# Two units of a rational activation in one instruction, on the steps that read SBUF alone

## The chip, the cores and the metric

The kernel runs on one NeuronCore of a Trainium2 chip. The metric is the device time of one execution in microseconds (us); a run's time is the median over its executions. The engines are TensorE (PE, with its weight loads PEld), VectorE (DVE), ScalarE (ACT) and GpSimd (POOL); SyncE (SP) only issues transfers. Each engine works through its own row of instructions in order. SBUF is the working memory with 128 partitions, PSUM holds matmul results in banks of 512 fp32 columns.

## The reference

A delta-rule attention (4 batches, 8 heads, 768 time steps, head size 48) is followed by a two-layer network with a rational activation (384 to 2048 to 384 columns, 3072 tokens):

```python
for t in range(S):
    y[:, :, t] = np.einsum('bhd,bhde->bhe', q[:, :, t], state)
    v_old = np.einsum('bhde,bhd->bhe', state, kt)
    state = state + bt * np.einsum('bhd,bhe->bhde', kt, vt - v_old)
...
h = x @ w_in
h2 = h * h
h3 = h2 * h
P = a[0] + a[1] * h + a[2] * h2 + a[3] * h3
Q = 1.0 + np.abs(b[0]) * np.abs(h) + np.abs(b[1]) * h2
g = P / (Q + 1e-06)
return g @ w_out
```

## The kernel before, in words

Time is cut into 12 chunks of 64 steps. For each chunk the attention is solved in blocks (the inverse of a triangular matrix in many small VectorE steps, the products on TensorE) and gives 256 tokens. They are transposed into `xT`, and the network runs on them.

The network walks over the hidden layer in units of two tiles of 128 hidden columns. A unit is 2 x 256 = 512 columns on 128 partitions, exactly one PSUM bank, and there are 8 units (`NU`) in a chunk, 96 in all. A unit n passes four functions:

- `hidden(n)`: 18 matmuls into one of two PSUM banks (`ps_h`, tile `ph`). Numbers are carried as pairs of fp16 (high and low part), so each product is three passes.
- `numerator(n)`: ScalarE computes `u = A3*h + a2` (L827) and `z = |B1*h|` (L829) from the bank, VectorE computes `u = h*u` (L830), `w = (z + B0)*h` (L832) and `u = (u + A1)*h` (L834), reading the bank each time. After L834 the bank is free. ScalarE then takes `w = |w|` (L833). In half the units of the chunks 2 to 10 GpSimd adds A0 to u (L838, `by_pool`).
- `quotient(n)`: ScalarE forms 1/Q as `exp(-ln(w + Q0))` (L845, L846, tile `r`). VectorE makes the high part `g = (u + A0)*r` in fp16 (L851, or L849 where GpSimd has added A0), then `w = (w + Q0)*g` (L852) and the remainder `u = u + A0 - w` (L856; in the `by_pool` units L854 on GpSimd). GpSimd makes the low part `u*r` (L857). All of these read SBUF only.
- `accumulate(n)`: 12 matmuls of g with `w_out` into `po` (L872). At the end of a chunk ScalarE scales `po` into `ob` (L886), and SP sends it out (L894).

The tiles u, r, w and g come from four tags, `mu`, `mr`, `mw`, `mg`, with three buffers (`MB`) each.

Before the first unit the weights are read as 64-bit floats and made into fp16 pairs (`load_in`, `load_out`, `to_f32`): SP loads a piece (L322) into a buffer of the tags mw, mu, mr in turn, ScalarE takes the absolute value (L325, into a buffer of `mg`), GpSimd clamps it (L326), VectorE shifts and joins the bits (L327, two L334). One scale is found for each unit.

The order of the instructions on each engine is fixed when the program is built, by a scheduler that sorts by priority and by a model of the times; the main loop interleaves one unit's numerator, the unit before's quotient and a piece of the attention of later chunks.

## Time and profile before

| | |
|---|---|
| median of 3 runs | 870.52 us (869.87 to 877.41) |
| span of the profiled execution | 875.0 us |
| VectorE busy | 797.9 us, 91% |
| TensorE busy | 629.4 us, 72% (weight loads 494.5 us) |
| ScalarE busy | 550.9 us, 63% |
| GpSimd busy | 469.5 us, 54% |
| first and last L827 | at 150.5 and 858.0 us |

Of the profiled execution only the span is known, from its first instruction to its last; it lies between the median and the slowest of the three runs. The rows of a page give a line, the engine, the operation, what it writes and reads, its shape and its count; behind the bar stand the busy time in us and the mean length of one in ns, then the idle time of the engine just before it and what ended that. The lengths of neighbours on VectorE overlap a little, so how long an instruction holds the queue is read from the next one's start.

### The profile page before, as it was taken

To read this page: it belongs to the slowest core of one execution; us is meant where nothing else is said; L and a number is where in the kernel's file an instruction comes from. 1 tells how busy PE (TensorE), PEld (TensorE's weight loads), DVE (VectorE), ACT (ScalarE), POOL (GpSimd) and SP (SyncE) were. 2 spreads that over 40 slices of the span, in tenths; PEclk is the share of its full clock that TensorE was granted. 3 is DMA by queue.
4 is the path that set the end of the run, shared out by engine and by line. 5 is a ranking of instruction groups with operands and counts; after the bars stand their busy time and mean duration, and the time that the engine had idled before them with its cause. 6 is when DMAs were issued, how large, how long until landed. Compare 5 with 4: busy or idle time off the path is not lost. (4 is left out here: it accounts for less than half of the span.)

```text
span 875.0 us, 23209 instructions
## 1 busy us (share of the span) xinstructions
PE 629.4 (72%) x9264; PEld 494.5 (57%) x9264; DVE 797.9 (91%) x1561; ACT 550.9 (63%) x1025; POOL 469.5 (54%) x430
## 2 busy tenths in 40 slices
PE   0230444875787688698778879788788878898885
PEld 0120344664565576576556667666566657676553
DVE  5999899899999789999989999999999898898996
ACT  4765675656466386585566678567576664868574
POOL 7655664537236447656646755654756444363622
PEclk9755556886999799899989989999999998999998
DMA  8987986679965987988689489597683824300000
GB/s 236 247 185 156 224 175 111 122 132 168 177 121 93 180 142 131 182 142 162 118 155 170 82 162 152 90 194 116 128 172 63 166 46 65 68 1 19 1 19 18
DMA packets 466507, 111.46 MB, mean 127 GB/s; under 512 B 431328, under 2 KB 463072, under 8 KB 466400
## 3 DMA queue, kind: packets, MB, share of 16 engines
q1 hardware_dynamic: 464224, 108.83, 66.8%
q8 instruction: 72, 1.18, 0.6%
q10 hardware_dynamic: 2176, 1.17, 0.4%
q14 instruction: 35, 0.29, 0.1%
HBM read 40.47 MB, written 26.23 MB: 76 GB/s over the span
## 5 line engine op out<-in xcount | busy, mean ns | idle before, releaser
L872 PE MATMUL po<-w_out,mg 128*128 128x384 f16 x1152 | 220.6, 339 | 42.2 <-POOL mg L857 33.7
L810 PE MATMUL ph<-xT,w_in 128*128 128x256 f16 x1728 | 221.5, 283 | 33.3 <-DVE mu L834 30.2
L810 PEld LDWEIGHTS <-w_in 128*128 128x128 f16 x1728 | 172.6, 102 | 70.5 <-DVE mu L834 22.4
L857 POOL TENSOR_TENSOR mg<-mu,mr 128x512 f16<-128x512 f32 x96 | 131.9, 1374 | 107.8 <-DVE mu L856 52.5
L872 PEld LDWEIGHTS <-mg 128*128 128x128 f16 x1152 | 109.7, 101 | 118.1 <-POOL mg L857 42.8
L827 ACT ACTIVATE mu<-ph,coef,msc 128x512 f32<-128x512 f32 x96 | 74.1, 772 | 50.4 <-POOL mg L857 17.3
L833 ACT ACTIVATE mw<-mw 128x512 f32<-128x512 f32 x96 | 60.3, 630 | 64.0 <-DVE mw L832 63.7
L852 DVE SCALAR_TENSOR_TENSOR mw<-mw,msc,mg 128x512 f32<-128x512 f32 x96 | 88.4, 922 | 0.4
L410 PEld LDWEIGHTS <-kbd 128*128 128x128 f16 x1680 | 61.7, 105 | 38.8 <-issue 36.2
L830 DVE TENSOR_TENSOR mu<-ph,mu 128x512 f32<-128x512 f32 x96 | 65.5, 683 | 17.1 <-ACT mr L829 13.4
L854 POOL TENSOR_TENSOR mu<-mu,mw 128x512 f32<-128x512 f32 x36 | 50.1, 1390 | 54.3 <-DVE mw L852 30.8
L832 DVE SCALAR_TENSOR_TENSOR mw<-mr,msc,ph 128x512 f32<-128x512 f32 x96 | 70.6, 736 | 0.0
L410 PE MATMUL pu<-z,ebd 128*128 128x48 f16 x1728 | 56.5, 188 | 19.4 <-DVE z L234 11.8
L834 DVE SCALAR_TENSOR_TENSOR mu<-mu,msc,ph 128x512 f32<-128x512 f32 x96 | 70.4, 733 | 0.0
L845 ACT ACTIVATE mr<-mw,msc 128x512 f32<-128x512 f32 x96 | 69.0, 720 | 1.8
L410 PEld LDWEIGHTS <-ebd 128*128 128x128 f16 x1728 | 55.3, 100 | 22.4 <-issue 20.9
L829 ACT ACTIVATE mr<-ph,msc 128x512 f32<-128x512 f32 x96 | 65.4, 681 | 0.0
L851 DVE SCALAR_TENSOR_TENSOR mg<-mu,msc,mr 128x512 f16<-128x512 f32 x60 | 61.5, 1024 | 2.3 <-ACT mr L846 2.3
L838 POOL TENSOR_SCALAR mu<-mu,msc 128x512 f32<-128x512 f32 x36 | 31.3, 869 | 56.3 <-DVE mu L834 50.2
L846 ACT ACTIVATE mr<-mr 128x512 f32<-128x512 f32 x96 | 60.2, 628 | 1.2
L856 DVE SCALAR_TENSOR_TENSOR mu<-mu,msc,mw 128x512 f32<-128x512 f32 x60 | 57.6, 960 | 0.2
L232 POOL TENSOR_TENSOR mm<-m,mm 128x1024 f16<-128x1024 f32 x12 | 30.3, 2527 | 44.2 <-ACT mm L228 36.0
(201 smaller groups left out, 1295.9 us busy)
## 6 DMA issues: line engine op xcount, KB each, us to landing
wsi<-in_moe_w_in_dram SPq DMA_DIRECT2D x24, 256.0 KB, 5.2
xdk<-kn SPq DMA_DIRECT2D x24, 256.0 KB, 3.6
kbd<-tk SPq DMA_DIRECT2D x24, 256.0 KB, 5.4
gd<-g SPq DMA_DIRECT2D x24, 256.0 KB, 3.4
wso<-in_moe_w_out_dram SPq DMA_DIRECT2D x32, 192.0 KB, 4.1
xdq<-kn SPq DMA_DIRECT2D x24, 256.0 KB, 3.4
mbd<-mm SPq DMA_DIRECT2D x24, 256.0 KB, 5.0
wc<-img SPq DMA_DIRECT2D x24, 256.0 KB, 4.9
```

The lines of the kernel that those rows point to most:

```text
L410: nc.tensor.matmul(dst[p][:, h], head(bd, lp, p * H + h), head(rt, rp, p * H + h), start=start and n == 0 and h == 0, stop=stop and n == l ...
L810: nc.tensor.matmul(ph[:, i], w_in[:, f2, wp, cc, i * P : (i + 1) * P], x[:, xp, cc], start=k == 0, stop=k == 3 * NCC - 1,)
L827: nc.scalar.activation(u, ph, AF.Identity, scale=A3, bias=a2)
L829: nc.scalar.activation(z, ph, AF.Abs, scale=B1)
L830: nc.vector.tensor_mul(u, ph, u)
L832: nc.vector.scalar_tensor_tensor(out=w, in0=z, scalar=B0, in1=ph, op0=ALU.add, op1=ALU.mult)
L834: nc.vector.scalar_tensor_tensor(out=u, in0=u, scalar=A1, in1=ph, op0=ALU.add, op1=ALU.mult)
L845: nc.scalar.activation(r, w, AF.Ln, bias=Q0)
L851: nc.vector.scalar_tensor_tensor(out=g[:, 0], in0=u, scalar=A0, in1=r, op0=ALU.add, op1=ALU.mult)
L852: nc.vector.scalar_tensor_tensor(out=w, in0=w, scalar=Q0, in1=g[:, 0], op0=ALU.add, op1=ALU.mult)
L857: nc.gpsimd.tensor_mul(g[:, 1], u, r)
L872: nc.tensor.matmul(po[p], g[:, gp, i, p * P : (p + 1) * P], w_out[:, f2, wp, i], start=f2 == lo and i == 0 and k == 0, stop=f2 == hi - 1 a ...
```

## The change

A unit is now four tiles of 128 hidden columns (`FT = 4`), 1024 columns, in two halves of one PSUM bank each. There are 4 units in a chunk and 48 in all; the halves are counted by `NS = 8`. `hidden`, the two ScalarE steps and the three VectorE steps on PSUM, and `accumulate` are done for one half at a time as before (now L839 to L843). The steps that read SBUF alone are done once for both halves: on ScalarE the absolute value (L855), the logarithm and the exponential (L858, L859), on VectorE L861 or L863, L864 and L868, on GpSimd L857, L866 and L869. Only in the very last unit they stay at one half each. The absolute value and GpSimd's L857 move from `numerator` into `quotient`. `quotient(m)` is called every second turn, after the next unit's first numerator, and `accumulate` comes three turns after its numerator instead of two.

The tags mu, mr, mw and mg hold 3, 3, 2 and 2 buffers of twice the size. The weights are loaded in the same units of four tiles: w_in in 12 pieces of 512 columns instead of 24 of 256, w_out in the same 32 pieces of 192; a scale is found for 4 units instead of 8. To make room, a zero tile is halved and sent twice, and a DMA scratch area is set to 1024 bytes.

```diff
+    FT = 4
+    NS = 8
+    MB = {"mu": 3, "mr": 3, "mw": 2, "mg": 2}
...
-    NU = NF // 2
+    NU = NF // FT
...
     def numerator(n):
-        c, f2 = divmod(n, NU)
-        d = unit[n]
+        m, half = divmod(n, 2)
+        c, f2 = divmod(m, NU)
...
+        if half == 0:
+            names = {"u": "mu", "r": "mr", "w": "mw"}
+            unit[m] = {x: sb.tile([P, FT, TG], F32, tag=t, name=f"{t}{m}", bufs=MB[t]) for x, t in names.items()}
+            unit[m].update(A0=A0, Q0=Q0, by_pool=2 <= c < NCH - 1 and f2 in (0, 2))
+        ph = hid.pop(n)
+        u, z, w = (unit[m][x][:, 2 * half : 2 * half + 2] for x in "urw")
         nc.scalar.activation(u, ph, AF.Identity, scale=A3, bias=a2)
         nc.scalar.activation(z, ph, AF.Abs, scale=B1)
         nc.vector.tensor_mul(u, ph, u)
         nc.vector.scalar_tensor_tensor(out=w, in0=z, scalar=B0, in1=ph, op0=ALU.add, op1=ALU.mult)
-        nc.scalar.activation(w, w, AF.Abs)
         nc.vector.scalar_tensor_tensor(out=u, in0=u, scalar=A1, in1=ph, op0=ALU.add, op1=ALU.mult)
-        by_pool = 2 <= c < NCH - 1 and f2 in (0, 4, 5, 6)
-        if by_pool:
-            nc.gpsimd.tensor_scalar(u, u, A0, 1.0, op0=ALU.add, op1=ALU.mult)
...
-    def quotient(n):
+    def quotient(m):
+        d = unit[m]
...
+        gs = d["g"] = sb.tile([P, 2, FT, TG], F16, tag="mg", name=f"mg{m}", bufs=MB["mg"])
+        step = 2 if m == NCH * NU - 1 else FT
+        for at in range(0, FT, step):
+            u, w, r = (t[:, at : at + step] for t in (us, ws, rs))
+            g = [gs[:, i, at : at + step] for i in range(2)]
+            nc.scalar.activation(w, w, AF.Abs)
+            if by_pool:
+                nc.gpsimd.tensor_scalar(u, u, A0, 1.0, op0=ALU.add, op1=ALU.mult)
+            nc.scalar.activation(r, w, AF.Ln, bias=Q0)
+            nc.scalar.activation(r, r, AF.Exp, scale=-1.0)
+            if by_pool:
+                nc.vector.tensor_mul(g[0], u, r)
+            else:
+                nc.vector.scalar_tensor_tensor(out=g[0], in0=u, scalar=A0, in1=r, op0=ALU.add, op1=ALU.mult)
+            nc.vector.scalar_tensor_tensor(out=w, in0=w, scalar=Q0, in1=g[0], op0=ALU.add, op1=ALU.mult)
+            if by_pool:
+                nc.gpsimd.tensor_sub(u, u, w)
+            else:
+                nc.vector.scalar_tensor_tensor(out=u, in0=u, scalar=A0, in1=w, op0=ALU.add, op1=ALU.subtract)
+            nc.gpsimd.tensor_mul(g[1], u, r)
...
-    N = NCH * NU
+    N = NCH * NS
     hidden(0)
-    for n in range(N + 2):
+    for n in range(N + 4):
         if n < N:
             numerator(n)
-        if 0 <= n - 1 < N:
-            quotient(n - 1)
-        attention(*divmod(n + SHIFT, NU))
-        if 0 <= n - 2 < N:
-            accumulate(n - 2)
+        if n > 0 and n % 2 == 0 and n <= N:
+            quotient(n // 2 - 1)
+        attention(*divmod(n + SHIFT, NS))
+        if 0 <= n - 3 < N:
+            accumulate(n - 3)
```

How the rows of instructions move is seen in the last chunk, where the network stands nearly alone. On VectorE before, with `mu91` the tile u of unit 91 and `ph_92` the bank of unit 92:

```order
L834 SCALAR_TENSOR_TENSOR mu91_13875<-mu91_13875,msc_11_13599,ph_91_13856 128x512
L851 SCALAR_TENSOR_TENSOR mg90_13886<-mu90_13826,msc_11_13599,mr90_13828 128x512
L852 SCALAR_TENSOR_TENSOR mw90_13831<-mw90_13831,msc_11_13599,mg90_13886 128x512
L830 TENSOR_TENSOR mu92_13922<-ph_92_13903,mu92_13922 128x512
L832 SCALAR_TENSOR_TENSOR mw92_13927<-mr92_13924,msc_11_13599,ph_92_13903 128x512
L856 SCALAR_TENSOR_TENSOR mu90_13826<-mu90_13826,msc_11_13599,mw90_13831 128x512
L834 SCALAR_TENSOR_TENSOR mu92_13922<-mu92_13922,msc_11_13599,ph_92_13903 128x512
```

And at the same place after, where `mu45` is the tile u of the unit of the banks 90 and 91, down to the program's end:

```order
L863 SCALAR_TENSOR_TENSOR mg45_13207<-mu45_13109,msc_11_12909,mr45_13110 128x1024
L841 TENSOR_TENSOR mu46_13199<-ph_93_13227,mu46_13199 128x512
L842 SCALAR_TENSOR_TENSOR mw46_13201<-mr46_13200,msc_11_12909,ph_93_13227 128x512
L864 SCALAR_TENSOR_TENSOR mw45_13111<-mw45_13111,msc_11_12909,mg45_13207 128x1024
L843 SCALAR_TENSOR_TENSOR mu46_13199<-mu46_13199,msc_11_12909,ph_93_13227 128x512
L841 TENSOR_TENSOR mu47_13282<-ph_94_13263,mu47_13282 128x512
L868 SCALAR_TENSOR_TENSOR mu45_13109<-mu45_13109,msc_11_12909,mw45_13111 128x1024
...
L863 SCALAR_TENSOR_TENSOR mg47_13346<-mu47_13282,msc_11_12909,mr47_13283 128x512 x2
L864 SCALAR_TENSOR_TENSOR mw47_13284<-mw47_13284,msc_11_12909,mg47_13346 128x512 x2
L868 SCALAR_TENSOR_TENSOR mu47_13282<-mu47_13282,msc_11_12909,mw47_13284 128x512 x2
```

The three wide steps of a unit lie between the narrow ones of the next two halves. In the last unit each of the three comes twice in a row.

On ScalarE in the same chunk before:

```order
L833 ACTIVATE mw91_13880<-mw91_13880 128x512
L827 ACTIVATE mu92_13922<-ph_92_13903,coef_99,msc_11_13599 128x512
L829 ACTIVATE mr92_13924<-ph_92_13903,msc_11_13599 128x512
L845 ACTIVATE mr91_13877<-mw91_13880,msc_11_13599 128x512
L846 ACTIVATE mr91_13877<-mr91_13877 128x512
```

And after:

```order
L839 ACTIVATE mu46_13199<-ph_92_13180,coef_99,msc_11_12909 128x512
L840 ACTIVATE mr46_13200<-ph_92_13180,msc_11_12909 128x512
L855 ACTIVATE mw45_13111<-mw45_13111 128x1024
L858 ACTIVATE mr45_13110<-mw45_13111,msc_11_12909 128x1024
L859 ACTIVATE mr45_13110<-mr45_13110 128x1024
L839 ACTIVATE mu46_13199<-ph_93_13227,coef_99,msc_11_12909 128x512
L840 ACTIVATE mr46_13200<-ph_93_13227,msc_11_12909 128x512
```

The three steps of a unit are now neighbours, and the two steps on the bank `ph_93` stand behind all three.

More of the change, by code (lines that the diff above doesn't have):

```diff
@@ L205 @@
         t = dfix.tile([P, BS], F32, name=f"img{i}")
-        nc.scalar.dma_start(out=t, in_=zero)
+        for half in range(2):
+            nc.scalar.dma_start(out=t[:, half * (BS // 2) : (half + 1) * (BS // 2)], in_=zero)
         img.append(t)
@@ L270, in scale_of @@
         return lg
-    NU = NF // 2
-    w_in = cpool.tile([P, NU, 2, NCC, 2 * P], F16, name="w_in")
-    w_out = cpool.tile([P, NU, 2, 2, DM], F16, name="w_out")
+    NU = NF // FT
+    w_in = cpool.tile([P, NU, 2, NCC, FT * P], F16, name="w_in")
+    w_out = cpool.tile([P, NU, 2, FT, DM], F16, name="w_out")
     sw = cpool.tile([P, 4, NU], F32, name="sw")
@@ L311, in staged @@
         stage[0] += 1
-        tag, bufs = STAGES[stage[0] % len(STAGES)]
-        return sb.tile(shape, dtype, tag=tag, name=nm, bufs=bufs)
+        tag = STAGES[stage[0] % len(STAGES)]
+        return sb.tile(shape, dtype, tag=tag, name=nm, bufs=MB[tag])
     gate = cpool.tile([P, 1], F32, name="gate")
@@ L374, in load_out @@
         nc.vector.tensor_mul(ss[:, 1:2], ro, ro)
-        for j in range(2):
-            if j == 0:
+        for j in range(FT):
+            if j % 2 == 0:
                 split16((w_out[:, i, 0, j], w_out[:, i, 1, j]), to[j].bitcast(F32), ss[:, 1:2])
@@ L795, in scalars @@
         d["ikap"][lo] = hi, ikap
+    hid = {}
     unit = {}
@@ L834, in numerator @@
         nc.vector.scalar_tensor_tensor(out=u, in0=u, scalar=A1, in1=ph, op0=ALU.add, op1=ALU.mult)
[L836 to L858 removed]
+    def quotient(m):
+        d = unit[m]
+        A0, Q0, by_pool = (d.pop(x) for x in ("A0", "Q0", "by_pool"))
+        us, ws, rs = (d.pop(x) for x in "uwr")
+        gs = d["g"] = sb.tile([P, 2, FT, TG], F16, tag="mg", name=f"mg{m}", bufs=MB["mg"])
[18 more added lines that the diff above has]
+            nc.gpsimd.tensor_mul(g[1], u, r)
@@ L860, in accumulate @@
     def accumulate(n):
-        c, f2 = divmod(n, NU)
-        g = unit.pop(n)["g"]
+        m, half = divmod(n, 2)
+        c, f2 = divmod(m, NU)
+        g = unit[m]["g"]
         lo = max(i for i in toks[c]["ikap"] if i <= f2)
         hi, ikap = toks[c]["ikap"][lo]
-        if f2 == lo:
+        if f2 == lo and half == 0:
             acc[c] = [ps_o.tile([P, DM], F32, tag=f"o{p}", name=f"po_{c}_{lo}_{p}") for p in PAIRS]
@@ L869, in accumulate @@
         for k, (gp, wp) in enumerate(sorted(PASSES)):
-            for i in range(2):
+            for i in (2 * half, 2 * half + 1):
                 for p in PAIRS:
@@ L876, in accumulate @@
                         start=f2 == lo and i == 0 and k == 0,
-                        stop=f2 == hi - 1 and i == 1 and k == len(PASSES) - 1,
+                        stop=f2 == hi - 1 and i == FT - 1 and k == len(PASSES) - 1,
                     )
+        if half == 0:
+            return
+        unit.pop(m)
         if f2 < hi - 1:
@@ L989 @@
     for what in ORDER:
-        for j in range(NU):
+        for j in range(NU if what in "wo" else NS):
             if what == "f":
```

63 lines of the change are left out of this document (22 added, 41 removed).

## The prediction

> **What bounds the kernel now.** I read the page's first part, then the engines' busy time by stage, then VectorE's waits, then the groups of instructions by line and shape.
>
> ```profile
> PE 629.4 (72%) x9264; PEld 494.5 (57%) x9264; DVE 797.9 (91%) x1561; ACT 550.9 (63%) x1025; POOL 469.5 (54%) x430
> 0.00:150.00 150.00, 45.84 (x723) 39.46 (x724) 133.38 (x363) 90.49 (x232) 92.62 (x129) 0.66 0.87 192
> 150.00:860.00 710.00, 576.97 (x8520) 451.99 (x8516) 657.85 (x1191) 457.33 (x788) 372.98 (x299) 0.94 0.65 116
> 860.00:875.00 15.00, 6.57 (x28) 3.02 (x28) 6.71 (x9) 3.03 (x5) 3.91 (x3) 0.83 0.11 26
> ```
>
> The second to fourth rows cut the span into the weight load, the main pass and the end; their columns are PE, PEld, DVE, ACT, POOL, the clock, the DMA share and GB/s. VectorE (DVE) is busy for 657.9 of the main pass's 710 us, 93%, and for 133.4 of the first 150. ScalarE (ACT) has 457 of 710, GpSimd (POOL) 373. So VectorE's queue sets the time, and an edit is worth what it takes out of that queue. The 52 us in which it stands are in small pieces:
>
> ```profile
> DVE mu L830 <- ACT mr L829: 13.4, 19, 1.6
> DVE mg L849 <- ACT mr L846: 3.1, 2, 2.4
> DVE mg L851 <- ACT mr L846: 2.3, 3, 1.0
> ```
>
> (us, times, longest.) The largest piece is the first VectorE step on a fresh PSUM bank, which waits for ScalarE's second step on it.
>
> **The merged steps on VectorE.** Per unit of 512 columns VectorE runs three steps on PSUM (L830, L832, L834), which stay, and the SBUF-only steps, which now come once per 1024:
>
> ```profile
> L852 DVE SCALAR_TENSOR_TENSOR mw<-mw,msc,mg 128x512 f32<-128x512 f32 x96 | 88.4, 922 | 0.4
> L851 DVE SCALAR_TENSOR_TENSOR mg<-mu,msc,mr 128x512 f16<-128x512 f32 x60 | 61.5, 1024 | 2.3 <-ACT mr L846 2.3
> L856 DVE SCALAR_TENSOR_TENSOR mu<-mu,msc,mw 128x512 f32<-128x512 f32 x60 | 57.6, 960 | 0.2
> L849 DVE TENSOR_TENSOR mg<-mu,mr 128x512 f16<-128x512 f32 x36 | 31.3, 868 | 4.4 <-ACT mr L846 3.1 <-POOL mu L838 1.4
> ```
>
> That is 216 scalar_tensor_tensor and 36 tensor_tensor, so 126 fewer; the last unit keeps its two halves, which gives 3 back. What one instruction less is worth I read from starts in the timeline (start, duration), since the queue overlaps neighbours:
>
> ```profile
> 850.70 0.75 DVE L851 SCALAR_TENSOR_TENSOR mg<-mu,msc,mr 128x512 f16<-128x512 f32 x1
> 851.36 0.75 DVE L856 SCALAR_TENSOR_TENSOR mu<-mu,msc,mw 128x512 f32<-128x512 f32 x1
> 852.03 0.69 DVE L830 TENSOR_TENSOR mu<-ph,mu 128x512 f32<-128x512 f32 x1
> 852.63 0.74 DVE L832 SCALAR_TENSOR_TENSOR mw<-mr,msc,ph 128x512 f32<-128x512 f32 x1
> ...
> 862.17 0.74 DVE L852 SCALAR_TENSOR_TENSOR mw<-mw,msc,mg 128x512 f32<-128x512 f32 x1
> 862.95 0.75 DVE L856 SCALAR_TENSOR_TENSOR mu<-mu,msc,mw 128x512 f32<-128x512 f32 x1
> ```
> ```profile
> 565.60 1.00 DVE L234 SCALAR_TENSOR_TENSOR sh<-S,sc,sh 128x768 f16<-128x768 f32 x1
> 566.53 0.24 DVE L511 RECIPROCAL nrm<-nrm 128x16 f32<-128x16 f32 x1
> ```
> ```profile
> 585.08 1.21 DVE L663 TENSOR_TENSOR m<-pm,mask 128x1024 f32<-128x1024 f32 x1
> 586.22 0.74 DVE L852 SCALAR_TENSOR_TENSOR mw<-mw,msc,mg 128x512 f32<-128x512 f32 x1
> 586.88 1.03 DVE L576 TENSOR_TENSOR pr<-ab,wt 128x512 f32<-128x512 f32 x1
> ```
>
> A scalar_tensor_tensor of 512 holds the queue for 0.66 us (850.70 to 851.36), one of 768 for 0.93 (565.60 to 566.53); 256 columns cost 0.27, so 1024 should take 1.20 and a pair saves 2 x 0.66 - 1.20 = 0.12. A tensor_tensor takes 0.60 at 512 and 1.14 at 1024 (585.08 to 586.22), a pair saves 0.06. The sum is 105 x 0.12 + 18 x 0.06 = 13.7 us. Where the next instruction reads the result (862.17 to 862.95) the step is 0.78, 0.12 more, and merging halves those places too: between 0 and 123 x 0.12 = 14.8 us more. In most places another instruction already stands between, so I take 2. Together 16 us, bounds 7 (0.06 for each of 123) and 28.
>
> The Trainium skill (Vector Engine (DVE) Microarchitecture Reference, section 5.2) gives about 75 ns of fixed cost per instruction once the queue overlaps; by it this term would be 126 x 0.075 = 9.5 us. The measured starts put it higher for scalar_tensor_tensor and near it for tensor_tensor.
>
> **The port between VectorE and GpSimd.** The same operation has two faces:
>
> ```profile
> L832 DVE SCALAR_TENSOR_TENSOR mw<-mr,msc,ph x96: 725/736/746, 152.5 to 860.1; 128x512 f32<-128x512 f32 x96
> L852 DVE SCALAR_TENSOR_TENSOR mw<-mw,msc,mg x96: 659/746/2158, 158.2 to 864.4; 128x512 f32<-128x512 f32 x96
> L849 DVE TENSOR_TENSOR mg<-mu,mr x36: 632/682/2124, 314.2 to 822.5; 128x512 f16<-128x512 f32 x36
> L857 POOL TENSOR_TENSOR mg<-mu,mr 128x512 f16<-128x512 f32 x96 | 131.9, 1374 | 107.8 <-DVE mu L856 52.5
> L854 POOL TENSOR_TENSOR mu<-mu,mw 128x512 f32<-128x512 f32 x36 | 50.1, 1390 | 54.3 <-DVE mw L852 30.8
> L838 POOL TENSOR_SCALAR mu<-mu,msc 128x512 f32<-128x512 f32 x36 | 31.3, 869 | 56.3 <-DVE mu L834 50.2
> L232 POOL TENSOR_TENSOR mm<-m,mm 128x1024 f16<-128x1024 f32 x12 | 30.3, 2527 | 44.2 <-ACT mm L228 36.0
> ```
>
> (Shortest, median, longest in ns.) With one input in PSUM it never strays from 746 ns; with both in SBUF the median is the same and the longest 2158, about one GpSimd instruction more. Against the medians (0.746, and 0.682 for L849) the four groups carry 16.8 + 16.7 + 12.8 + 6.7 = 53 us of such stretch. Of GpSimd's 373 us in the main pass 213 are the unit's own three steps, which also double in width (2.5 us at 1024, by L232), 160 the attention's, which don't. I share the stretch likewise: 30 and 23. Half as many meetings with steps twice as long leave the 30; half as many with unchanged steps save 11.5. Against that stand VectorE's unmerged two-input steps:
>
> ```profile
> L576 DVE TENSOR_TENSOR pr<-ab,wt 128x512 f32<-128x512 f32 x12 | 19.2, 1602 | 0.0
> L794 DVE TENSOR_TENSOR msc<-tab,sf 128x48 f32<-128x48 f32 x11 | 6.7, 606 | 1.0 <-DVE sf L258 0.5
> L794 DVE TENSOR_TENSOR msc<-tab,sf 128x24 f32<-128x24 f32 x2 | 0.3, 168 | 0.0
> ```
>
> L576 runs 1.03 when free (586.88 above) and 1.60 on average, 6.8 us over 12; L794 0.44 too long, 4.8 over 11. With the smaller groups I estimate 22 us in all; 57% of it, 12.5, meets the widened steps and doubles. Net about +1, taken as 0, bounds -11.5 and +12.5.
>
> **The weight load.** w_in comes in 12 pieces of 512 instead of 24 of 256, so 24 L334 and 12 L327 go, and the small scale steps run for 4 units instead of 8. One L334 of 256 columns costs little more than its data:
>
> ```profile
> 26.18 0.41 DVE L334 SCALAR_TENSOR_TENSOR w_out<-wsi,w_out 128x256 uint32<-128x256 uint32 x1
> 26.52 0.14 DVE L352 TENSOR_SCALAR wss<-wss 128x1 f32<-128x1 f32 x1
> 26.58 0.28 DVE L327 TENSOR_SCALAR w_out<-wai 128x256 uint32<-128x256 uint32 x1
> ```
>
> 0.34 less 0.27 of columns is 0.07, times 36, plus some 28 small steps at 0.06 (26.52 to 26.58): 4 us, at most 8. The other way, the staging tags mw and mg have two buffers instead of three; VectorE stands 16.6 us in this stage, and a third more of that would cost 6. I take -4.
>
> **ScalarE and the tail.** Its three SBUF steps merge as well; it is not the bound, so their saving counts for nothing. But they now form one block:
>
> ```profile
> L833 ACT ACTIVATE mw<-mw 128x512 f32<-128x512 f32 x96 | 60.3, 630 | 64.0 <-DVE mw L832 63.7
> L845 ACT ACTIVATE mr<-mw,msc 128x512 f32<-128x512 f32 x96 | 69.0, 720 | 1.8
> L846 ACT ACTIVATE mr<-mr 128x512 f32<-128x512 f32 x96 | 60.2, 628 | 1.2
> L526 ACT ACTIVATE g<-pg 128x1024 f32<-128x1024 f32 x12 | 12.2, 1020 | 11.3 <-PE pg L410 8.8 <-DMA knbd<-xdk 2.5
> ```
>
> 2.0 us becomes about 3.2 (three at 1.02 to 1.15), and the first two steps on the next PSUM bank may queue behind it. If the waits of L830, L849 and L851 (18.8 us) grow by 3.2/2.0, that is +11; since ScalarE also has less to do, I take +3, bounds -3 and +11. At the end the last quotient is two halves as before, but both L863 now stand ahead of both L864; about +1.
>
> **Sum.** -16 - 4 + 0 + 3 + 1 = -16 against the span of 875.0, so 859. The runs' median is 870.5 (869.9 to 877.4), 4.5 below that span; the same 16 us gives 854.5.
>
> **Rivals.** *The port takes it back.* GpSimd's two steps L866 and L869 follow each other in the 18 units that use it, 5 us in which VectorE's in-order queue can be stopped at any two-input step. For it: the longest L852 stands 1.4 us over its median, a whole GpSimd step, and that step doubles. Against: merging halves the meetings. With this term at its bound, -16 + 12.5 = -3.5 gives 867, within 1%; with ScalarE's term at its bound too (+8 over what I took) 875. The Trainium skill (SBUF — State Buffer, Who interferes with whom) says that whoever issues first gets the shared port for its whole instruction and the other blocks, and that a VectorE instruction with two SBUF inputs is such a one; the rows agree, and by that rule wider GpSimd steps speak against this change.
>
> *ScalarE's block starves VectorE* (the slower side). There are two PSUM banks for the hidden layer. If a bank's first two ScalarE steps stand behind the 3.2 us block, VectorE's L841 stands too, and everything behind it. It decides from 16/48 = 0.33 us per pair of units; at 0.65 us, a fifth of the block, it costs 31 us in place of the +3 above and gives 870.5 - 19 + 31 = 882. Its own range is 876 to 900, the latter at 1 us per pair. For it: L830's wait for L829 is already the largest. Against: 19 waits in 96 units, and ScalarE is busy for 64% of this stage.
>
> **Numbers.** Forecast 0.60, the port 0.25, the block 0.13, something else 0.02. A measurement of this kernel tells about 1% from no change, 8.7 us. Faster by more than that 0.60, within 0.25, slower 0.15. The range goes down to the merged steps at their bound with half of the port's gain (-28 - 4 - 6 + 3 + 1 = -34) and up to the port's case with both terms at their bounds (+5): 836 to 876; only the block's case and what is unlikelier lie outside.
>
> **What would show it.** L863, L864 and L868 near 1.28 us at the median, 30 to 49 of each; VectorE busy for some 640 us in the main pass, standing 50 to 57; the sum of stretch on the merged rows near 40. Wrong if the medians are right and L583, L566 or L801 take twice as long as L576, L559, L794 (the port), or if L841's wait for L840 goes past 30 us (the block).

## The result, and the profile after

The changed kernel takes 896.0 us (median of 4 runs, 895.3 to 899.7), the kernel before 870.2 us beside it (867.8 to 877.4): 1.029 times as long, 95% interval 1.023 to 1.034. The profiled execution took 895.3 us, its span is 893.5.

The page's first part and the three stages again (columns as before):

```profile
PE 637.3 (71%) x9251; PEld 501.4 (56%) x9252; DVE 769.0 (86%) x1374; ACT 521.0 (58%) x840; POOL 455.2 (51%) x335
```
```profile
0.00:150.00 150.00, 47.07 (x718) 39.01 (x719) 126.81 (x283) 81.84 (x181) 89.28 (x112) 0.89 0.89 190
150.00:860.00 710.00, 569.46 (x8394) 449.12 (x8395) 618.10 (x1067) 424.06 (x641) 355.96 (x218) 0.91 0.68 116
860.00:894.00 34.00, 20.78 (x141) 13.22 (x139) 24.06 (x25) 15.10 (x21) 9.91 (x5) 0.98 0.05 12
```

VectorE has 28.9 us less to do (797.9 to 769.0), and so have ScalarE (30) and GpSimd (14). But VectorE now stands 893.5 - 769.0 = 124.5 us, against 77.1 before: 47.4 us of new idle time for 28.9 saved, and the difference, 18.5, is what the span grew by. (The span of the kernel before, 875.0 us, is longer than three of its four runs, and the changed kernel's profiled execution is the shortest of its four; so the spans differ by 18.5 us where the medians differ by 25.8.) In the main pass it stands 92 us of 710, before 52.

The merged steps have the lengths that were expected at the median (groups by shape; then the three lines by themselves, with the shortest, median and longest in ns, where the 512-element forms are the last unit's):

```profile
L864 DVE SCALAR_TENSOR_TENSOR mw<-mw,msc,mg 128x1024 f32<-128x1024 f32 x47 | 76.5, 1628 | 0.2
L868 DVE SCALAR_TENSOR_TENSOR mu<-mu,msc,mw 128x1024 f32<-128x1024 f32 x29 | 44.7, 1541 | 0.1
L863 DVE SCALAR_TENSOR_TENSOR mg<-mu,msc,mr 128x1024 f16<-128x1024 f32 x29 | 43.1, 1485 | 6.4 <-ACT mr L859 4.0 <-PE po L883 2.0 <-ACT sf L796 0.2
L861 DVE TENSOR_TENSOR mg<-mu,mr 128x1024 f16<-128x1024 f32 x18 | 21.9, 1219 | 1.4 <-issue 0.8 <-PE po L883 0.2
L583 DVE TENSOR_TENSOR pr<-ab,wt 128x512 f32<-128x512 f32 x12 | 17.5, 1456 | 0.0
L801 DVE TENSOR_TENSOR msc<-tab,sf 128x24 f32<-128x24 f32 x11 | 9.0, 820 | 0.5
```
```profile
L864 DVE SCALAR_TENSOR_TENSOR mw<-mw,msc,mg x49: 739/1279/3447, 159.6 to 882.2; 128x1024 f32<-128x1024 f32 x47, 128x512 f32<-128x512 f32 x2
L868 DVE SCALAR_TENSOR_TENSOR mu<-mu,msc,mw x31: 739/1276/3243, 162.3 to 883.6; 128x1024 f32<-128x1024 f32 x29, 128x512 f32<-128x512 f32 x2
L863 DVE SCALAR_TENSOR_TENSOR mg<-mu,msc,mr x31: 737/1284/3261, 158.2 to 880.9; 128x1024 f16<-128x1024 f32 x29, 128x512 f16<-128x512 f32 x2
```

The waits that stand out (us, times, longest) are those of VectorE for ScalarE's second step on a bank, 13.4 us before, and of ScalarE for a bank filled by the hidden matmuls:

```profile
DVE mu L841 <- ACT mr L840: 30.4, 26, 3.0
DVE m L670 <- PE pm L417: 9.3, 4, 5.2
DVE z L237 <- ACT z L233: 8.5, 8, 2.5
ACT mu L839 <- PE ph L818: 50.8, 25, 7.2
```

So the work went as planned, and the time did not follow it.

### The profile page after: what moved, and what is told of

The parts are those of the page before. It is cut to its first block, busy times and chain, and to the rows that moved or that the text cites. A ratio compares the mean times of both kernels' runs of the same rounds, so it can differ in the third digit from the quotient of the medians.

```text
span 893.5 us, 22553 instructions
## 1 busy us (share of the span) xinstructions
PE 637.3 (71%) x9251; PEld 501.4 (56%) x9252; DVE 769.0 (86%) x1374; ACT 521.0 (58%) x840; POOL 455.2 (51%) x335
## 4 chain that ended last, share of the span: by engine, by line
DVE 28%; DMA 19%; PE 18%; SPq 13%; ACT 9%; issue 8%; POOL 4%; ACTq 0%; DVEq 0%; POOLq 0%
PE ph L818 6%; PE po L883 5%; SPq L121 4%; DMA kbd<-tk 3%; DVE mw L864 3%; DVE w_out L337 2%; DVE mg L863 2%; DMA tk<-xdk 2%; DVE mu L868 2%; DMA tq<-xdq 2%; DVE mu L841 2%; SPq L455 2%; DMA q<-in_q_dram 2%; DMA wbd<-wc 2%; DMA k<-in_k_dram 2%
## 5 line engine op out<-in xcount | busy, mean ns | idle before, releaser
L883 PE MATMUL po<-w_out,mg 128*128 128x384 f16 x1152 | 211.4, 337 | 24.4 <-POOL mg L869 16.5
L869 POOL TENSOR_TENSOR mg<-mu,mr 128x1024 f16<-128x1024 f32 (+1 forms) x49 | 120.3, 2456 | 81.3 <-DVE mu L868 42.3
L839 ACT ACTIVATE mu<-ph,coef,msc 128x512 f32<-128x512 f32 x96 | 74.3, 774 | 71.0 <-PE ph L818 50.8
L841 DVE TENSOR_TENSOR mu<-ph,mu 128x512 f32<-128x512 f32 x96 | 65.6, 684 | 30.8 <-ACT mr L840 30.4
L866 POOL TENSOR_TENSOR mu<-mu,mw 128x1024 f32<-128x1024 f32 x18 | 43.9, 2440 | 85.1 <-DVE mw L864 65.9
L864 DVE SCALAR_TENSOR_TENSOR mw<-mw,msc,mg 128x1024 f32<-128x1024 f32 (+1 forms) x49 | 77.9, 1592 | 0.2
L855 ACT ACTIVATE mw<-mw 128x1024 f32<-128x1024 f32 (+1 forms) x49 | 51.0, 1041 | 46.3 <-DVE mw L842 46.2
L843 DVE SCALAR_TENSOR_TENSOR mu<-mu,msc,ph 128x512 f32<-128x512 f32 x96 | 70.5, 735 | 0.0
L840 ACT ACTIVATE mr<-ph,msc 128x512 f32<-128x512 f32 x96 | 65.5, 682 | 0.0
L417 PEld LDWEIGHTS <-wbd 128*128 128x128 f16 x1152 | 37.8, 101 | 49.2 <-issue 43.4
L235 POOL TENSOR_TENSOR mm<-m,mm 128x1024 f16<-128x1024 f32 x12 | 30.4, 2537 | 58.5 <-ACT mm L231 58.4
L858 ACT ACTIVATE mr<-mw,msc 128x1024 f32<-128x1024 f32 (+1 forms) x49 | 55.5, 1132 | 1.0
L863 DVE SCALAR_TENSOR_TENSOR mg<-mu,msc,mr 128x1024 f16<-128x1024 f32 (+1 forms) x31 | 46.2, 1494 | 6.4 <-ACT mr L859 4.0
L859 ACT ACTIVATE mr<-mr 128x1024 f32<-128x1024 f32 (+1 forms) x49 | 50.8, 1037 | 0.7
L868 DVE SCALAR_TENSOR_TENSOR mu<-mu,msc,mw 128x1024 f32<-128x1024 f32 (+1 forms) x31 | 46.1, 1489 | 0.1
```

The source lines that it names most:

```text
L417: nc.tensor.matmul(dst[p][:, h], head(bd, lp, p * H + h), head(rt, rp, p * H + h), start=start and n == 0 and h == 0, stop=stop and n == l ...
L839: nc.scalar.activation(u, ph, AF.Identity, scale=A3, bias=a2)
L840: nc.scalar.activation(z, ph, AF.Abs, scale=B1)
L841: nc.vector.tensor_mul(u, ph, u)
L843: nc.vector.scalar_tensor_tensor(out=u, in0=u, scalar=A1, in1=ph, op0=ALU.add, op1=ALU.mult)
L863: nc.vector.scalar_tensor_tensor(out=g[0], in0=u, scalar=A0, in1=r, op0=ALU.add, op1=ALU.mult)
```

## The experiments

Times are medians; where a ratio is given, it is to the kernel before on the same chip, with its 95% interval. "VectorE alone wide" stands below for the last form of the first group.

**First group: which part of the change costs.** The changed kernel's weights, buffers and tiles, with the old loop on them:

```diff
-    for n in range(N + 4):
+    for n in range(N + 2):
...
-        if n > 0 and n % 2 == 0 and n <= N:
-            quotient(n // 2 - 1)
+        if 0 <= n - 1 < N:
+            quotient(n - 1)          # one half, 512 elements
...
-        if 0 <= n - 3 < N:
-            accumulate(n - 3)
+        if 0 <= n - 2 < N:
+            accumulate(n - 2)
```

> This keeps the changed kernel's weights (four tiles to a unit, fewer and larger loads), its buffers and its tiles, and puts back the loop of the kernel before: the steps on SBUF at 512 elements, one half at a time, one turn behind the numerator, the accumulation two turns behind. Theory 'coarse work starves VectorE' (the 47 us of new idle time come from handing work over two units at a time): 866 to 874 us, VectorE idle back near 77 us. Theory 'weights, buffers and their queues' (the cause lies outside the loop): 888 to 900 us. Theory 'luck of the order' (any edit perturbs the order that the scheduler writes out, by some 10 us either way): anything from 865 to 890, with idle time in other chunks than before.

Then the grouping kept and each step 512 wide (`step = 2` for all units), only ScalarE's steps narrow, and only VectorE's steps wide:

> This keeps the changed kernel's grouping (the quotient of both halves called every second turn, the accumulation three turns behind), and makes each instruction on SBUF 512 elements wide again. VectorE's busy time must come back to about 798 us in all. Theory 'ScalarE's and VectorE's wide blocks': the waits shrink (L841 for L840 from 30 us to below 18), 868 to 878 us. Theory 'grouping itself' (deferral to every second turn and the longer lag, whatever the width): the idle time stays near 124 us and the saved 29 us are lost as well, 905 to 925 us. Theory 'weights and buffers': 888 to 925.

> Only ScalarE's three steps on SBUF (Abs, Ln, Exp) go back to 512 elements; VectorE's and GpSimd's steps stay at 1024, grouping and lag stay. Theory 'ScalarE's wide block': ScalarE can put the next bank's Identity and Abs between the narrow steps, L841's wait for L840 falls from 30 us to about 13 to 18 and PE's side of it (ScalarE waiting for the hidden matmuls, 51 us) falls too, VectorE keeps its saving: 858 to 875 us. Theory 'grouping itself': within 6 us of the changed kernel, 890 to 902 us, since the order of the work is the same.

> Only VectorE's steps on SBUF stay at 1024 elements; ScalarE's and GpSimd's go back to 512, grouping and lag stay. Theory 'ScalarE's wide block': as with ScalarE narrow alone, 858 to 875 us. Theory 'the shared port': GpSimd's narrow steps take more turns at the port against VectorE's wide ones, VectorE's standing time grows by 10 to 25 us over the run with ScalarE narrow alone. Theory 'grouping itself': 890 to 902 us, and if GpSimd's wide step adds to it (accumulation starting late because both halves of g1 come in one 3 us step), 5 to 10 us below the run with ScalarE narrow alone.

In the last two the three engines' loops over a unit stand one behind the other, with a step of their own each:

```diff
-        for at in range(0, FT, step):
-            u, w, r = (t[:, at : at + step] for t in (us, ws, rs))
+        for u, w, r, g0, g1 in pieces(2):      # ScalarE: Abs, Ln, Exp
+            ...
+        for u, w, r, g0, g1 in pieces(4):      # VectorE
+            ...
+        for u, w, r, g0, g1 in pieces(2):      # GpSimd; 4 where only ScalarE is narrow
+            ...
```

Measured: 888.2 us (1.020, 1.013 to 1.026) with the old loop, 893.8 (1.025, 1.019 to 1.030) all narrow, 894.4 (1.026, 1.021 to 1.030) with ScalarE narrow, 897.1 (1.030, 1.025 to 1.035) with VectorE alone wide. The first row of the page of the all-narrow run:

```profile
PE 643.5 (72%) x9251; PEld 510.8 (57%) x9252; DVE 803.5 (90%) x1497; ACT 544.3 (61%) x981; POOL 481.3 (54%) x418
```

VectorE has 34.5 us more to do than in the changed kernel, and the time is the same within the intervals. So in this surrounding the width is worth nothing that shows: 893.8 us with no wide step, 897.1 with VectorE's, 894.4 with VectorE's and GpSimd's, 896.0 with all. ScalarE's wide block isn't what costs either: with its steps narrow the time was to come out at 858 to 875. The waits of L841 for L840 say the same. Here they are with the old loop, all narrow, with ScalarE narrow and with VectorE alone wide, against 30.4 us in the changed kernel:

```profile
DVE mu L841 <- ACT mr L840: 12.6, 17, 1.5
```
```profile
DVE mu L841 <- ACT mr L840: 16.6, 19, 2.4
```
```profile
DVE mu L841 <- ACT mr L840: 28.1, 23, 4.3
```
```profile
DVE mu L841 <- ACT mr L840: 23.3, 27, 2.4
```

(us, times, longest.) The wait was to fall to 13 to 18 us with ScalarE narrow and stayed at 28.1, and at 23.3 with GpSimd narrow too, so the wide block isn't what makes it long; and where it is short, the time is hardly better: the five times lie within 9 us of one another. "Grouping itself" had 890 to 902 us for the last two runs, which holds, but 905 to 925 for all narrow, which doesn't. Two thirds of the loss, 17 us, is there with the old loop and without one wide step; "luck of the order" and "weights and buffers" both allow that.

**Second group: the two halves apart, and the order.** The attention left out (the tokens are the loaded queries), for the kernel before, the changed kernel and VectorE alone wide; and the kernel before with a single number changed:

```diff
-            with tc.high_priority(300):
+            with tc.high_priority(330):
```

> The kernel before without its attention: the tokens of each chunk are the loaded queries, copied by ScalarE; the delta rule's inversions, products, transposes and DMAs are left out, the network and the loading of its weights stay. It is the base for the next two runs: seven units take 27.9 us in the last chunk of the kernel before, 4.0 us a unit, so the steady pace should be 31 to 34 us a chunk, with VectorE busy nearly all the time; some 450 to 500 us in all.

> The changed kernel without its attention, in the same manner. Theory 'coarse work starves VectorE': the steady pace is no better than that of the kernel before without attention, or worse, by 0 to 2 us a chunk (last chunk 29.6 against 27.9 us), with VectorE idle at L841 in every chunk: 0 to 25 us longer in all. Theory 'the order beside the attention' (the merge itself is a gain; what is lost is lost where the attention's chain and the network share engines in a written-out order): the pace gains what the start-to-start times gain, about 1.4 us a chunk (16 us over 12 chunks), 12 to 22 us shorter in all.

> The run with only VectorE's steps wide (ScalarE and GpSimd at 512), without attention, in the same manner. If ScalarE's and GpSimd's wide steps are what starves VectorE: 1 to 3 us a chunk faster than the changed kernel without attention (over its last three chunks the run with the attention took 108.3 us against 118.0 of the changed kernel and 114.2 of the kernel before), so 12 to 36 us shorter. If grouping alone does it, no difference beyond 5 us.

> The kernel before, untouched in every instruction, with one number changed: the attention's steps are put ahead by 330 places instead of 300 in the order that the scheduler writes out. Theory 'the order that was found is special' (any edit that moves the order costs 10 to 20 us, the change among them): 878 to 892 us, with new idle time of VectorE between 300 and 750 us. Theory 'the loss belongs to this change': 866 to 875 us.

Without the attention the kernel before takes 589.7 us, the changed kernel 578.8, VectorE alone wide 557.6. The merge is a gain there, of 11 and of 32 us, and the first VectorE step on a bank shows the pace: 95 units from its first start to its last (the last two numbers ahead of the shape), in 480.2, 461.0 and 445.3 us, 40.4, 38.8 and 37.5 us a chunk. (My 31 to 34 us a chunk and 450 to 500 us in all were too low.) One row for each kernel:

```profile
L831 DVE TENSOR_TENSOR mu<-ph,mu x96: 672/683/692, 93.6 to 573.8; 128x512 f32<-128x512 f32 x96
```
```profile
L842 DVE TENSOR_TENSOR mu<-ph,mu x96: 662/682/692, 92.8 to 553.8; 128x512 f32<-128x512 f32 x96
```
```profile
L842 DVE TENSOR_TENSOR mu<-ph,mu x96: 668/680/693, 92.1 to 537.4; 128x512 f32<-128x512 f32 x96
```

So the loss needs the attention beside the network. (The changed kernel's gain of 11 us is 1 short of the 12 to 22 expected; 40.4 to 38.8 us a chunk is 1.6, for some 1.4 expected.) Here, where nothing else is in the way, ScalarE's and GpSimd's wide steps do cost, 21 us together. Part of it shows on VectorE's product in the units in which GpSimd adds A0, in the changed kernel and with VectorE alone wide:

```profile
L862 DVE TENSOR_TENSOR mg<-mu,mr 128x1024 f16<-128x1024 f32 x18 | 39.4, 2187 | 2.4 <-POOL mu L858 2.4
```
```profile
L870 DVE TENSOR_TENSOR mg<-mu,mr 128x1024 f16<-128x1024 f32 x18 | 26.0, 1447 | 3.3 <-ACT mr L864 1.7 <-POOL mu L867 1.5
```

0.74 us more, 18 times, is 13 us on this line. Over all lines VectorE is only 5.9 us busier (506.4 against 500.5); the rest of the 19.6 us between the two spans is idle time, and its wait for ScalarE's second step on a bank is 19.0 us against 11.6. In the traces the product is long where one of GpSimd's two-input steps runs beside it. At 302 us in the changed kernel without the attention, 2.28 us of GpSimd's step are left when the product starts, and the product takes 2.1 us longer than the 1.22 that it takes alone:

```profile
302.41 2.34 POOL L870 TENSOR_TENSOR mg<-mu,mr 128x1024 f16<-128x1024 f32 x1
302.47 3.36 DVE L862 TENSOR_TENSOR mg<-mu,mr 128x1024 f16<-128x1024 f32 x1 [0.52 <-POOL mu L858]
```

By my count, 16 of the 18 products meet such a step there (1.49 to 3.37 us, the other two 1.22), and 5 of 18 with VectorE alone wide (1.70 to 2.28 us, the others 1.21 to 1.23).

The new number in the order brought the kernel before to 864.8 us (0.990, 0.984 to 0.995), better than either theory allowed: the order it had wasn't the best to be found.

**Third group: the attention alone, the weights alone, and the new number in the changed forms.** The first leaves the network out of the kernel before. The second takes the old loop on the new weights and gives each half unit tiles of its own again:

```diff
-            unit[m] = {x: sb.tile([P, FT, TG], F32, tag=t, name=f"{t}{m}", bufs=MB[t]) for x, t in names.items()}
...
+        u, z, w = unit[m][half] = [
+            sb.tile([P, 2, TG], F32, tag=t, name=f"{t}{n}", bufs=MB[t]) for t in ("mu", "mr", "mw")
+        ]
```

> The kernel before without the network: the hidden matmuls, the rational function and the second matmul are left out, the attention's result goes straight to the output; the loading of the weights stays. In the kernel before the tokens of a chunk come within 4 us of the network's first matmul on them in chunks 0 to 6, so the network waits for the attention there. Theory 'the attention's own chain sets the pace of chunks 1 to 8': it takes 50 us a chunk or more alone, over 650 us in all. Theory 'the two only hinder each other in the order written out': 25 to 40 us a chunk, 400 to 550 us in all.

> The run with the loop of the kernel before on the changed kernel's weights (888 us) with the last thing of the change's tiles taken out: each half unit has its own 512-element tiles again, three buffers of each, released half by half; the weights are staged in two tile kinds instead of three. What is left of the change is the new form of the weights. Theory 'weights': 884 to 892 us as before. Theory 'tiles released only in pairs': 866 to 876. Theory 'the order found is luck': neither of these need hold, 860 to 890, and the difference to the run with the paired tiles lies in the chunks that run beside the attention (0 to 8), not in the last three.

> The changed kernel with the attention's steps 330 places ahead instead of 300. The kernel before gained 1% (7.7 us) by it. Theory 'the loss belongs to the change': it stays some 26 us behind the kernel before at the same number, 885 to 897 us. Theory 'the order found is luck': the distance between the two kernels changes by 10 us or more in either direction, with the difference in chunks 0 to 8.

> Only VectorE's steps wide, ScalarE's and GpSimd's at 512, with the attention's steps 330 places ahead instead of 300. Without attention this form was 32 us faster than the kernel before, with it 26 us slower. Theory 'the order found is luck': 850 to 885 us, the gain where chunk 2 no longer stands (92 us there at 300, 70 in the kernel before). Theory 'the deferral holds the attention up whatever the order': 890 to 900 us.

The attention alone takes 684.0 us. Its result for a chunk, y, is copied from PSUM by ScalarE; the row gives the first and the last of the 12 starts, and the second the share of 16 DMA engines' time that its main queue fills:

```profile
L726 ACT ACTIVATE y<-py,sc x12: 882/898/902, 128.0 to 672.6; 128x768 f32<-128x768 f32 x12
```
```profile
q1 hardware_dynamic: 464224, 108.83, 87.4%
```

That is (672.6 - 128.0) / 11 = 49.5 us a chunk, more than the network's 40.4. In the kernel before the two together take 61.0 us a chunk, (798.1 - 127.5) / 11. So the attention is the longer strand of the two, and I had looked at the network alone. In the run of the attention alone, half of the chain that ended last is SP's issuing of transfers and the transfers themselves, and VectorE is busy for 57% of the span:

```profile
SPq 30%; DVE 23%; DMA 21%; PE 10%; ACT 8%; issue 6%; POOL 2%; ACTq 0%; DVEq 0%; POOLq 0%
```

(The granted TensorE clock from 150 to 700 us is 0.62 in that run and 0.92 in the kernel before. So 49.5 us may be somewhat long, but TensorE is only 10% of the chain.)

The new weights without paired tiles take 880.0 us (1.009, 1.006 to 1.011), 8 us below the old loop on paired tiles and 8 above the kernel before; that fits neither "weights" nor "tiles", and "luck" (860 to 890) allows it. This run still has the halved zero tile and the smaller DMA scratch area, and no run took these apart from the weights. At 330 the changed kernel takes 894.1 (1.024, 1.017 to 1.031) and VectorE alone wide 884.1 (1.013, 1.007 to 1.019). The kernel before had gained 7.7 there: the changed kernel is 29 us behind it at that number and VectorE alone wide 19, at 300 they are 26 and 26. The distance moves by less than the 10 us that "luck" asked for, though 884.1 us by itself lies in the range of "luck" for that run (850 to 885) and not in that of the deferral (890 to 900).

**Fourth group: the attention further ahead, in both.** Once the whole attention is called one turn earlier (`SHIFT = 3` for 2), once all its steps are put 300 places ahead:

```diff
             if cc < NCH:
-                f(cc, j)
+                with tc.high_priority(300):
+                    f(cc, j)
```

> The kernel before with the whole attention called one turn earlier against the network (three turns ahead instead of two). It is the base for the next run. Theory 'the attention's chain sets the pace beside the network': 860 to 872 us, since the kernel before has its attention only just in time (tokens within 4 us of their first use in chunks 0 to 6), and an earlier call helps a little. Theory 'the order found is luck': anything from 855 to 895.

> Only VectorE's steps wide, and the whole attention called one turn earlier. Theory 'the attention's chain sets the pace beside the network, and the grouped network delays it': an earlier call gives the chain its place back, chunks 1 and 2 fall from 175 us to below 155, and the distance to the kernel before with the same call falls from 26 us to 10 or less: 855 to 880 us. Theory 'the deferral holds the attention up whatever the order': 885 to 900 us.

> The kernel before with every step of the attention put 300 places ahead, not only those of the solution and the state (the keys' and queries' loading, the inversion, the scales and the tokens are added). Base for the next run. Theory 'the attention's chain sets the pace': 855 to 870 us. If the network is then held up by attention steps that nobody needs yet: 875 to 900.

> Only VectorE's steps wide, with every step of the attention put 300 places ahead. Theory 'the attention's chain sets the pace, and the grouped network delays it': VectorE's step on wt in chunk 3 (276 us here against 239 us in the kernel before) comes back by 20 us or more, the time falls by 20 us or more from 897: 845 to 877 us. Theory 'the deferral holds the attention up whatever the order': 885 to 900 us.

One turn earlier the kernel before takes 888.7 (1.021, 1.014 to 1.027) and VectorE alone wide 908.3 (1.042, 1.036 to 1.048); with the attention first 874.5 (1.003, 1.000 to 1.007) and 891.2 (1.021, 1.015 to 1.027). The distances are 19.6 and 16.7 us. Of the expectations, only "luck" has the 888.7 and only the deferral the 891.2; the 874.5 falls between two ranges, and the 908.3 lies above every range. In four orders VectorE alone wide lies 17 to 26 us behind the kernel before in the same order. That speaks against "luck" as the whole of the loss, and against the hope that the attention only had to be put ahead. It isn't excluded that another order suits the merged forms: none was searched for, and the changed kernel itself was measured at 300 and 330 alone.

That the kernel before lost 17 us by an earlier call was a surprise, and its trace held a wait that could explain it. The attention's y and the network's output ob share one buffer. In the kernel before, ob of chunk 1 is asked for ahead of y of chunk 3. One turn later for the accumulation, or one earlier for the attention, and y comes first: then the copy of chunk 1's sums out of PSUM waits until chunk 3's tokens have been made from y, and no sum of chunk 2 can start. In the timeline of the kernel before the copy (L886) follows 1.2 us behind the start of chunk 1's last matmuls:

```profile
294.03 1.46 PE L872 MATMUL po<-w_out,mg 128*128 128x384 f16 x4 [3.88 <-POOL mg L857]
295.21 1.05 ACT L886 ACTIVATE ob<-po,kp 128x384 f32<-128x384 f32 x2 [5.92 <-PE po L872]
314.98 1.31 PE L872 MATMUL po<-w_out,mg 128*128 128x384 f16 x7
```

In the changed kernel it comes 56 us after the last matmul, beside the steps that make chunk 3's tokens (xT):

```profile
307.48 0.48 PE L883 MATMUL po<-w_out,mg 128*128 128x384 f16 x2
...
363.68 1.03 ACT L900 ACTIVATE ob<-po,kp 128x384 f32<-128x384 f32 x2
364.60 0.90 ACT L233 ACTIVATE xT<-px,sf 128x768 f16<-128x768 f32 x1
365.42 1.14 PE L883 MATMUL po<-w_out,mg 128*128 128x384 f16 x6
```

**Fifth group: the shared buffer.** The two calls exchanged, in the changed kernel and in VectorE alone wide at 330:

```diff
-        attention(*divmod(n + SHIFT, NS))
         if 0 <= n - 3 < N:
             accumulate(n - 3)
+        attention(*divmod(n + SHIFT, NS))
```

> The changed kernel with two calls in the loop exchanged: the accumulation (three turns behind) comes ahead of the attention of that turn, not behind it. All instructions stay. What it changes: the attention's result y of a chunk and the network's output ob of the chunk before the last share one buffer (tag ob, one of it). In the kernel before, ob of chunk 1 is asked for ahead of y of chunk 3; with the accumulation a turn later, in the same turn but behind the attention, y of chunk 3 is asked for first, so that the copy of chunk 1's sums out of PSUM waits until the tokens of chunk 3 have been made from y: the traces show waits of 18 to 87 us between the last matmul of a chunk's sums and that copy in every run with the later accumulation (changed kernel 56, 31, 22, 36 us for chunks 1 to 4) and in the kernel before with the attention a turn earlier (69, 18, 29, 24), against 0 to 4 us in the kernel before. Theory 'the shared buffer changed hands': waits of 5 us or less, chunk 2 from 79 back below 72 us, 855 to 872 us. Theory 'the attention's chain alone sets the pace': the waits go and the time stays within 8 us of 896. Theory 'ScalarE's wide block starves VectorE': L841's waits for L840 stay at 25 us or more and the time above 885.

> Only VectorE's steps wide, ScalarE's and GpSimd's at 512, the attention's steps 330 places ahead (884 us so), and the accumulation called ahead of the attention in its turn as in the run beside it. Theory 'the shared buffer changed hands': 835 to 860 us, faster than the kernel before (872) and than the kernel before at 330 (865), with chunk 2 near 70 us against 90. Theory 'the attention's chain alone sets the pace': 875 to 890 us.

The wait went: the copy starts 1.7 us after the start of the last matmuls in the changed kernel. (The 18 to 87 us of the expectation are 15 to 92 if VectorE alone wide with the attention first is counted too.)

```profile
305.65 0.48 PE L883 MATMUL po<-w_out,mg 128*128 128x384 f16 x2
307.35 1.07 ACT L900 ACTIVATE ob<-po,kp 128x384 f32<-128x384 f32 x2
```

VectorE's busy time between 300 and 400 us came back in part, in the changed kernel from the first row to the second, with VectorE alone wide at 330 from the third to the fourth; the kernel before (the fifth) has 90.9:

```profile
300.00:400.00 100.00, 72.98 (x1270) 60.44 (x1267) 76.30 (x150) 55.19 (x88) 49.25 (x35) 0.88 0.79 134
```
```profile
300.00:400.00 100.00, 80.57 (x1361) 65.13 (x1359) 82.03 (x143) 60.91 (x97) 52.51 (x36) 0.91 0.81 144
```
```profile
300.00:400.00 100.00, 70.78 (x1239) 59.49 (x1238) 67.76 (x123) 54.45 (x95) 46.14 (x41) 0.85 0.93 143
```
```profile
300.00:400.00 100.00, 77.19 (x1298) 62.63 (x1296) 77.17 (x129) 62.24 (x108) 47.54 (x38) 0.90 0.90 147
```
```profile
300.00:400.00 100.00, 80.80 (x1398) 66.58 (x1397) 90.93 (x161) 68.44 (x118) 58.05 (x47) 0.95 0.85 146
```

The time hardly did: 891.0 us (1.023, 1.017 to 1.028) and 882.2 (1.012, 1.007 to 1.016), 5 and 2 us less, within the intervals. The shared buffer was a real wait of 56 us for one copy, and at most a few us of the loss. Of the theories, "the attention's chain alone sets the pace" held in both runs. "ScalarE's wide block" had its numbers in the first too (L841 waits 33.0 us for L840 there, and the time is above 885), but the first group had taken the growth of that wait away without getting the time back.

**What all runs with the attention have in common** is in one row of each, the start of the last y. Of the kernel before, the changed kernel, VectorE alone wide (at 300, then at 330), and the changed kernel with the calls exchanged:

```profile
L726 ACT ACTIVATE y<-py,sc x12: 880/896/905, 127.5 to 798.1; 128x768 f32<-128x768 f32 x12
```
```profile
L733 ACT ACTIVATE y<-py,sc x12: 882/896/933, 123.3 to 811.5; 128x768 f32<-128x768 f32 x12
```
```profile
L733 ACT ACTIVATE y<-py,sc x12: 881/894/902, 121.2 to 822.1; 128x768 f32<-128x768 f32 x12
```
```profile
L733 ACT ACTIVATE y<-py,sc x12: 881/894/900, 119.4 to 805.6; 128x768 f32<-128x768 f32 x12
```
```profile
L733 ACT ACTIVATE y<-py,sc x12: 882/900/901, 120.7 to 805.5; 128x768 f32<-128x768 f32 x12
```

| kernel | time | span | VectorE busy | last y at | span less that |
|---|---|---|---|---|---|
| before, 330 | 864.8 | 863.0 | 789.2 | 786.3 | 76.7 |
| before | 870.2 | 875.0 | 797.9 | 798.1 | 76.9 |
| before, attention first | 874.5 | 870.4 | 794.0 | 792.5 | 77.9 |
| before, one turn earlier | 888.7 | 886.0 | 796.9 | 807.5 | 78.5 |
| new weights alone | 880.0 | 878.2 | 791.4 | 801.1 | 77.1 |
| old loop, new weights, paired tiles | 888.2 | 887.7 | 804.9 | 809.1 | 78.6 |
| grouped, all narrow | 893.8 | 892.1 | 803.5 | 816.0 | 76.1 |
| changed, ScalarE narrow | 894.4 | 890.9 | 774.7 | 809.0 | 81.9 |
| changed | 896.0 | 893.5 | 769.0 | 811.5 | 82.0 |
| changed, 330 | 894.1 | 893.1 | 777.2 | 811.2 | 81.9 |
| changed, calls exchanged | 891.0 | 887.7 | 777.5 | 805.5 | 82.2 |
| VectorE alone wide | 897.1 | 896.6 | 766.8 | 822.1 | 74.5 |
| the same, 330 | 884.1 | 880.1 | 755.7 | 805.6 | 74.5 |
| the same, 330, calls exchanged | 882.2 | 880.8 | 764.7 | 802.7 | 78.1 |
| the same, one turn earlier | 908.3 | 906.8 | 772.5 | 827.4 | 79.4 |
| the same, attention first | 891.2 | 890.6 | 762.5 | 794.7 | 95.9 |

In 15 of 16 the kernel ends 74 to 82 us after the last y (the network then has the rest of chunk 10 and chunk 11 before it), while the last y itself moves by 41 us and VectorE's busy time by 49, the one with the time and the other not. In the changed kernel 13.4 of the span's 18.5 us lie ahead of the last y and 5.1 behind it. The four kernels with a wide GpSimd step have the 82.

In the changed kernel most of this arises early. By the traces' starts, VectorE's first step on a bank of chunk 2 comes at 307 us in both kernels, on one of chunk 3 at 376 in the kernel before and at 387 in the changed kernel, and on one of chunk 11 at 832 and at 846: of 14 us, 11 come in chunk 2, while the copy of chunk 1's sums waits. With the calls exchanged it is 379 for chunk 3 and 841 for chunk 11: of the 9 us lost there, 3 come in chunk 2 and 6 later.

What stays open: what in the new form holds the attention back. That it ends later is measured. That it is the cause and not carried along by a slower network is argued from the network's speed without it and from its own 684 us; both strands stand in the same rows, and a delay of either can delay the other. One thing speaks against it as the only cause: in the changed kernel the tokens of the chunks 3, 4 and 6 to 9 are ready 9 to 11 us before the network's first matmul on them (in the kernel before at most 1 us ahead, but 6.6 for chunk 7), so the network isn't waiting for the attention there. With VectorE alone wide at 330 and the calls exchanged they come within 3 us again in the chunks 2 to 9, and that kernel is still 9 us slower than the kernel before. The ladder of the first and third groups (870 before, 880 with the new weights, 888 with paired tiles, 894 with grouping, 896 with width) is measured in one order only, and single steps of 8 us are no more than a change of order made in the kernel before. No version with merged steps was faster than the kernel before; the kernel before at 330 beats both.

## Why the prediction was wrong

The forecast was 854.5 us, and slower by more than 1% had a chance of 0.15. The step that failed is the first: "VectorE's queue sets the time, and an edit is worth what it takes out of that queue". What the runs showed in its place: taking 34.5 us out of that queue was worth nothing (the grouped kernel with narrow and with wide steps, 803.5 and 769.0 us of VectorE's work for 893.8 and 896.0 us). VectorE's 93% in the main pass was made up of two strands, and of these the attention, which the merge doesn't touch, is the longer one by itself (684.0 us against 589.7). And beside the weight load the sum had no term for what else the change does than widen steps: the paired tiles, the later accumulation, the smaller scratch area. With the old loop and no wide step, 17 of the 26 us of loss were already there. Which of these costs what, and why, stays open. The 7.7 us that a shift of the order gave the kernel before show that time was to be had in the order.

Point by point:

- **Merged steps, -16.** Right as work: medians of 1.28 us as forecast. VectorE's busy time in the main pass fell by 39.8 us to 618, more than the "some 640", but that window now also holds 16 us less of the pass, since the network ends later. It stands for 92 us there, not for the 50 to 57 that would have shown the step to be right. Over the whole span it fell by 28.9, and without the attention the span's main stretch shortens by 19 to 35 us. It was worth nothing in the full kernel.
- **Weight load, -4.** The stage has 6.6 us less for VectorE (133.4 to 126.8), yet the first step on a bank starts at 151.2 us for 151.9; by my count over the trace's rows 6.5 us of weight steps now lie behind that start, 0.5 before. Worth 0.7. With the old loop and single tiles (and the weights staged in two kinds of buffers) what changed outside the loop, the weights' new form, the halved zero tile and the smaller scratch area, costs 8 us rather than saving 4.
- **Port, 0.** The merged rows' stretch over their medians was to be near 40 us; by the rows above it is (1.628 - 1.279) x 47 + (1.541 - 1.276) x 29 + (1.485 - 1.284) x 29 = 30. L583 fell from 1.60 to 1.46 us, L801 rose from 0.61 to 0.82 at half the elements, and the mean of L566 from 0.44 to 0.49 over its three shapes; none doubled. So the port didn't take the gain back here. Without the attention the 13 us on L862 show what meetings with GpSimd's wide steps can cost one line.
- **ScalarE's block, +3, bound +11.** The waits grew by 17 us at L841 alone, past the 30 that I had named as the sign of the rival. But the rival is not the cause: with the wait at 12.6 and at 16.6 us the time was 888 and 894. That its range, 876 to 900, holds the time is luck. Where the network stands alone it may be a part of the 21 us: the wait is 19.0 us in the changed kernel and 11.6 with VectorE alone wide.
- **Tail, +1.** From the last first step on a bank to the end it is 2.6 us more (859.5 to 875.0 before, 875.4 to 893.5 after), from the last y to the end 5.1; the kernels with wide GpSimd steps have the most there but for one.
- **The Trainium skill's** fixed cost of about 75 ns an instruction (Vector Engine (DVE) Microarchitecture Reference, section 5.2) would have given 9.5 us, an estimate, for a term that was measured as work and was worth nothing as time: the choice between 9.5 and 16 didn't matter.

What the prediction lacked as a rival is a second strand that is as long as the first. The profile of before held signs of it. While the attention runs, DMA is busy for 0.79 of its engines' time beside VectorE's 510 of 550 us (the window's last two columns are the DMA share and GB/s):

```profile
150.00:700.00 550.00, 438.01 (x6871) 347.45 (x6868) 510.30 (x946) 346.82 (x603) 306.01 (x246) 0.92 0.79 141
```

And by the trace's starts the tokens of the chunks 0 to 6 were made within 4 us of the network's first matmul on them. I had read the waits only by their length, as small pieces.

## What to carry to other kernels

That an engine is busy for 93% of a stage doesn't show that it sets the time; where two chains of work share it, take each alone on the chip before pricing an edit of one of them. Price an edit that regroups work by what else it reorders, too: which of two tiles asks first for a shared buffer turned round here with a call that came one turn later, and the trace showed it as waits of 22 to 56 us (chunks 1 to 4 of the changed kernel). And when a saving shows as idle time, vary the order in both kernels: a distance that stays (17 to 26 us in four orders) is hardly luck alone, and a single number in the order can be worth more than the edit (7.7 us).
